# Neighbourhood attention on one core: two more tiles for turned probabilities, one store on another queue, and another split of V's shift

## The chip, the cores and the metric

The kernel runs on one core of a Trainium2 chip. The metric is the time of one execution on the device, in microseconds (us). Of the kernel before three runs are shown; their median is 342.44 us.

## The reference

The input is an image of 224 x 224 pixels with 192 channels in bfloat16. Each pixel attends to a 7 x 7 neighbourhood with a dilation of 2, clipped at the edges.

```python
qkv = x @ wqkv
r0 = jnp.clip(ir - half, 0, H - 1 - (ks - 1) * dil)      # ks 7, dil 2, half 6
c0 = jnp.clip(ic - half, 0, W - 1 - (ks - 1) * dil)
logits = jnp.einsum('bnc,bnkc->bnk', qf, kn) * scale     # kn, vn: keys and values of the 49 neighbours
p = _softmax(logits, axis=-1)
o = jnp.einsum('bnk,bnkc->bnc', p, vn) @ wo
```

## The kernel before

With a dilation of 2 a pixel only meets pixels of its own row parity and column parity. So the image falls into classes: the row class `rc` is 0 or 1, and the two column classes `cc` are worked on side by side. The work goes in 14 steps (`NSTEP`), for seven bands of 16 rows and the two row classes in turn. A step has seven pairs of slots; a slot is 16 rows by 8 columns, 128 queries of each column class. There are 98 pairs, counted by `k`; `n` is the step, `m` the pair in the step, `s = 2m` or `2m + 1` the slot (0 to 13).

The projections are folded together: G holds x times (wq wk^T), so that the scores are G against x itself, and V holds x times (wv wo), so that the last product is the output. Of the image, XA and XB hold channels and marks that make the softmax's window; x arrives by transposing DMAs (line 154), one third of it through the tiles of pool `x1` (two buffers), from which GpSimd copies it to XB (`xb_items`, line 160) and, sorted, to XS (`sort_items`, line 170).

A pair passes these stages:

- `stage1` (lines 499, 501): TensorE (PE) multiplies G with the window of x to scores in PSUM; VectorE (DVE) takes the negative maximum.
- `stage1b` (line 508): ScalarE (ACT) writes the exponentials, in bfloat16, to one of three tiles `p`.
- `stage2`: the probabilities are turned, to tile `pt_sb` (three buffers). Mostly PE does it (line 535) and DVE or ACT copies the result out of PSUM (line 536). The pairs in the table `TURN` are turned by a transposing DMA on SP's queue (line 519): the pair `m = 5` of steps 2 to 10, pairs 2 to 6 of steps 11 and 12, pairs 0 and 1 of step 13.
- `stage3` (line 545): PE multiplies the turned probabilities with V; a column of ones gives the sum.
- `stage4` (lines 551, 566, 568): DVE or ACT divides, and the output is stored (lines 574, 585, 597).

The order is written out by hand, and `in_order` keeps each engine's instructions in the order of the program. The loop over `k` emits `stage1` of pair k, then `stage3` and part of `stage4` of pair k - 3 (`values_of`), then the second half of `stage1b`, then `stage2` (at once for a pair turned by DMA, a pair later for the others).

Beside the pairs runs the work for the next step, by the tables `BACK` and, from k = 80 on, `LATE`: seven strings, one for each pair, naming blocks of V (`v0` to `v13`), parts of G (`g`) and the half parts of G (`h`), whose result GpSimd copies in place (line 450). The first entry of a string goes ahead of the second exponential, the others behind it.

V is kept twice: `stage3` of the upper half of the rows needs the lower half of V's partitions (0 to 63) in the other one of two tiles. `v_over` (line 349) copies it for a range of the 14 blocks. `back` calls it, when the block of a list has been made: after block 7 for blocks 0 to 7, after block 10 for 8 to 10, after block 13 for 11 to 13. It is a DMA on SP's queue, and in steps 11 and 12 (`nb >= 11`) a copy on GpSimd.

In the last step `stage4` puts the outputs of all slots into one tile (`xs`), and each slot from 1 on is stored with one DMA for 12 rows: slot 13 from ACT's queue, the others from SP's (line 574). The other four rows are stored as short stores over several slots (line 585): four on GpSimd after slot 7, four at the very end from the list `end_q`. GpSimd also stores slot 0 of every step in many small pieces (line 597), some of them after each pair.

SP's DMAs wait in order for what they need, and each also for the DMA eight places earlier, since eight semaphores go round.

Of the kernel before, what the change touches and what calls it, by code (L numbers as in the profile page):

```python
# [8 lines left out]
BF = mybir.dt.bfloat16  # L9
# [12 lines left out]
NSLOT = 14  # L22
# [5 lines left out]
BND = 16 * S  # L28
# [13 lines left out]
def _aff_runs(vals):  # L42
    out = []
    i, n = 0, len(vals)
    while i < n:
        j = i
        step = 1
        if i + 1 < n and vals[i + 1] > vals[i]:
            step = vals[i + 1] - vals[i]
            j = i + 1  # L50
            while j + 1 < n and vals[j + 1] - vals[j] == step:
                j += 1
        out.append((i, j - i + 1, vals[i], step))
        i = j + 1
    return out


def _rows(rc, ti):

    return [_phys(rc, 16 * ti + j) for j in range(16)]  # L60
# [7 lines left out]
def _win(t, p0, pn, off, dims):  # L68
    a = t[:]
    ps = a.ap[0][0]  # L70
    return bass.AP(a.tensor, a.offset + p0 * ps + off, [[ps, pn]] + [list(d) for d in dims])
# [18 lines left out]
def in_order(tc):  # L90

    last = {}
    for i in tc.nc.cur_bb.bb.instructions:
        if i.engine in last:
            tc.add_manual_dep(i, last[i.engine], mybir.DependencyInfo(mybir.DependencyClass.NoSync, mybir.DependencyReason.DATA), reason="program order")
        last[i.engine] = i.name
# [3 lines left out]
def kernel(  # L100
# [7 lines left out]
    nc = tc.nc  # L108
# [12 lines left out]
    x1_p = ctx.enter_context(tc.tile_pool(name="x1", bufs=2))  # L121
# [199 lines left out]
    work = ctx.enter_context(tc.tile_pool(name="work", bufs=2))  # L321
# [25 lines left out]
    def v_over(rc, ti, c0, c1, eng=nc.sync.dma_start):  # L347

        eng(out=VV[rc][1 - ti % 2][0:64, c0:c1, :], in_=VV[rc][ti % 2][0:64, c0:c1, :])
# [163 lines left out]
    def turned(J):  # L513
        return J.m in TURN[J.n]

    def stage2(J):
        J.pt = work.tile([128, 8, 128], BF, name="pt_sb", tag="pt_sb", bufs=3)
        if turned(J):
            nc.sync.dma_start_transpose(out=J.pt[:], in_=J.p[:].rearrange("p a c q k -> p (a c q k)"))
            return  # L520
        if J.k == NP - 1:

            for ab in range(2):
                pt_ps = ps_g.tile([128, 4, 128], BF, name="pt_ps", tag="pg")
                for i in range(4):
                    for h in range(2):
                        nc.tensor.transpose(pt_ps[64 * h:64 * h + 64, i, :], J.p[:, ab, i // 2, i % 2, 64 * h:64 * h + 64], ident[:])
                nc.vector.tensor_copy(out=J.pt[:, 4 * ab:4 * ab + 4, :], in_=pt_ps[:])
            return
        pt_ps = ps_t.tile([128, 8, 128], BF, name="pt_ps", tag="pt")  # L530
        for ab in range(2):
            for cc in range(2):
                for q in range(2):
                    for h in range(2):
                        nc.tensor.transpose(pt_ps[64 * h:64 * h + 64, 4 * ab + 2 * cc + q, :], J.p[:, ab, cc, q, 64 * h:64 * h + 64], ident[:])  # L535
        (nc.scalar.copy if J.n == NSTEP - 1 and 2 <= J.m < 5 else nc.vector.tensor_copy)(out=J.pt[:], in_=pt_ps[:])  # L536
# [12 lines left out]
    def stage4a(J, ab):  # L549
        J.rs[ab] = stat.tile([128, 2], F32, name="rs", tag="rs")  # L550
        nc.vector.reciprocal(out=J.rs[ab][:], in_=J.o_ps[ab][:, C:C + 2])  # L551
        return J.rs[ab]

    def stage4(J, ab):
        rc, ti, s, o_ps = J.rc, J.ti, 2 * J.m + ab, J.o_ps[ab]
        rs = J.rs.get(ab) or stage4a(J, ab)
        if s > 0 and J.n == NSTEP - 1:

            o_sb = _win(XS[0], 0, 128, 2 * C * s, [[C, 2], [1, C]])
        elif s > 0:  # L560
            o_sb = work.tile([128, 2, C], BF, name="o_sb", tag="o_sb", bufs=6)
        else:
            o_sb = work.tile([128, 2, C], BF, name="o_s0", tag="o_s0")
        if J.k >= NP - 3 and ab == 1:
            for cc in range(2):
                nc.scalar.mul(o_sb[:, cc, :], o_ps[:, 194 * cc:194 * cc + C], rs[:, cc:cc + 1])
        else:
            nc.vector.tensor_tensor(out=o_sb[:], in0=_win(o_ps, 0, 128, 0, [[194, 2], [1, C]]),  # L568
                                    in1=rs[:].unsqueeze(2).to_broadcast([128, 2, C]), op=ALU.mult)
        prow = _rows(rc, ti)  # L570
        if s > 0:
            for (j0, nj, r0, rstep) in _aff_runs(prow) if J.n < NSTEP - 1 else [(0, 12, prow[0], 2), (12, 1, prow[12], 1), (13, 3, prow[13], 2)]:
                def put(eng, j0=j0, nj=nj, r0=r0, rstep=rstep):
                    eng.dma_start(out=op[r0: r0 + (nj - 1) * rstep + 1: rstep, 8 * s - 3:8 * s + 5, :],
                                  in_=o_sb[8 * j0:8 * (j0 + nj)].rearrange("p t c -> p (t c)"))

                if J.n < NSTEP - 1:
                    put(nc.gpsimd if nj < 8 and s % 2 == 1 else nc.sync)
                elif nj >= 8:
                    put(nc.scalar if s == NSLOT - 1 else nc.sync)  # L580
                elif s in SHORT:

                    for j in range(nj):
                        def row(eng, p=8 * (j0 + j), r=r0 + j * rstep, a=SHORT[s]):
                            eng.dma_start(out=op[r, 8 * a - 3:8 * s + 5, :].rearrange("(t i) c -> i t c", i=8),
                                          in_=_win(XS[0], p, 8, 2 * C * a, [[2 * C, s + 1 - a], [1, 2 * C]]))
                        if s < NSLOT - 1:
                            row(nc.gpsimd)
                        else:
                            end_q.append(row)  # L590
            return
        for h in range(2):
            for (j0, nj, r0, rstep) in _aff_runs(prow[8 * h:8 * h + 8]):
                for (cc, i0, n, mem, pair) in ((0, 0, 3, 1, 0), (0, 3, 5, 0, 0), (1, 6, 2, 1, 3), (1, 0, 3, 1, 109), (1, 3, 3, 0, 109)):
                    p = 64 * h + 8 * j0 + i0 * nj
                    dst = op[r0: r0 + (nj - 1) * rstep + 1: rstep, pair:pair + n, mem * C:(mem + 1) * C]
                    pool_q.append(lambda dst=dst, p=p, m=n * nj, cc=cc: nc.gpsimd.dma_start(out=dst.rearrange("j i c -> i j c"), in_=o_sb[p:p + m, cc, :]))  # L597
# [3 lines left out]
    for n, (ti, rc) in enumerate(steps):  # L601
        for m in range(7):
            J = Pair()
# [94 lines left out]

    def back(it, by_dve):
        it(by_dve)  # L700
        for (i, c0, c1) in ((7, 0, 8), (10, 8, 11), (13, 11, 14)):
            if it in vs and it is vs[i]:
                v_over(rcb, tib, c0, c1, pool if nb >= 11 else nc.sync.dma_start)

# [6 lines left out]
    for k in range(NP + 2):  # L711
        J = pairs[k] if k < NP else None
# [21 lines left out]
        if k == NP:  # L734
            stage2(pairs[k - 1])
        late = [pairs[i] for i in values_of(k)]
        for A in late[:1]:
            stage3(A, 0)
            stage3(A, 1)
            if k >= NP:  # L740
                stage4a(A, 0)
                stage4a(A, 1)
            stage4(A, 0)
            if k == NP - 1:
                stage4a(A, 1)
        for (it, by_dve) in w64:
            back(it, by_dve)
        if J:
            stage1b(J, 1)
        if J and turned(J):  # L750
            stage2(J)
        if 1 <= k < NP and not turned(pairs[k - 1]):
            stage2(pairs[k - 1])

        if late and n > 0:
            stage4(late[0], 1)
        for A in late[1:]:
            stage3(A, 0)
            stage3(A, 1)
            stage4(A, 0)  # L760
            stage4(A, 1)
# [15 lines left out]
        for (it, by_dve) in w128:  # L777
            back(it, by_dve)
# [22 lines left out]
        pool_do(max(4 if n < NSTEP - 1 else 8, len(add)))  # L801
    pool_do(len(pool_q))
    for (q, it) in enumerate(end_q):
        it((nc.scalar, nc.sync)[q % 2])
    in_order(tc)


# [28 lines left out]
```

## Time and profile before

| | us |
|---|---|
| runs shown: lowest, median, highest | 341.17, 342.44, 344.3 |
| the profiled execution | 345.27 |
| its span, first to last instruction | 343.5 |
| mean granted clock of TensorE in it | 0.998 of full speed |

The span is the time between the first and the last instruction in the trace. A row of a group has the source line, engine, operation, tile written and tiles read, sizes, count, busy time, the mean of one, and the idle time before it with what ended it. A row of the timeline has start, time, engine, line and operation, and how many instructions are merged in it. SPq, ACTq and POOLq stand for the sequencers, which issue DMAs or wait. A row of waits has the engine and line that waited, what it waited for, the sum, the number of times and the longest.

### The profile page before, as it was taken

How to read it: one execution, taken by the hardware profiler on the slowest of the kernel's cores; microseconds unless marked ns; L12 is line 12 of the kernel's file. 1: busy time of each engine (PE TensorE's matmuls, PEld its weight loads, DVE VectorE, ACT ScalarE, POOL GpSimd, SP SyncE). 2: the span in 40 equal slices, each digit the busy share in tenths (PEclk: the TensorE clock that was granted, in tenths of full speed). 3: DMA queues.
4: the chain of work that ended last, by engine and by line, in shares of the span. 5: the costliest groups of instructions: out<-in, count | busy, mean ns of one | idle time of the engine just before them, and what ended most of it. 6: DMA issues, size and time to landing. Idle time of an engine off the chain costs nothing.

```text
span 343.5 us, 19147 instructions
## 1 busy us (share of the span) xinstructions
PE 321.3 (94%) x7964; PEld 295.1 (86%) x7964; DVE 311.4 (91%) x730; ACT 311.7 (91%) x816; POOL 288.2 (84%) x447
## 2 busy tenths in 40 slices
PE   4599999999999999999999999999999999899882
PEld 2478898899899999999999989899999999798771
DVE  8759999899999999989999999899999999799892
ACT  6679899999999999989999999999999999899982
POOL 8399999999989969699598895996969939998592
PEclk9999999999999999999999999999999999999999
DMA  8999645978999996896898979979898667769934
GB/s 173 212 169 209 132 100 123 223 177 195 181 177 167 175 195 155 160 196 141 165 173 166 202 160 165 155 164 176 178 193 182 138 136 119 140 112 111 174 87 98
DMA packets 135685, 55.43 MB, mean 161 GB/s; under 512 B 108717, under 2 KB 132826, under 8 KB 135599
## 3 DMA queue, kind: packets, MB, share of 16 engines
q1 hardware_dynamic: 129555, 51.63, 78.7%
q0 software_dynamic: 5328, 1.75, 2.9%
q8 instruction: 62, 1.02, 1.3%
q10 hardware_dynamic: 716, 0.84, 1.2%
q14 instruction: 24, 0.20, 0.2%
HBM read 0.29 MB, written 19.27 MB: 57 GB/s over the span
## 4 chain that ended last, share of the span: by engine, by line
PE 72%; ACT 7%; DMA 7%; DVE 6%; SPq 3%; issue 3%; DVEq 0%; ACTq 0%
PE s L499 16%; PE o_ps L545 15%; PE pg L415 11%; PE pv L335 8%; PE pt_ps L535 8%; PE pv L338 7%; PE pgh L415 6%; DMA pt_sb<-p 5%; ACT p L508 4%; SPq L154 3%; DVE nmx L501 3%; DMA xa<-in_x_dram 2%; ACT v L328 1%; ACT gx L328 1%; ACT g L328 1%
## 5 line engine op out<-in xcount | busy, mean ns | idle before, releaser
L508 ACT ACTIVATE p<-s,nmx 128x256 bf16<-128x256 f32 x392 | 163.1, 483 | 16.4 <-DVE nmx L501 14.1
L501 DVE TENSOR_REDUCE nmx<-s 128x2 f32<-128x448 f32 (+1 forms) x196 | 114.5, 624 | 12.1 <-PE s L499 6.9
L568 DVE TENSOR_TENSOR o_sb<-o_ps,rs 128x384 bf16<-128x384 f32 x169 | 94.2, 557 | 6.3 <-DVE rs L551 0.3
L499 PEld LDWEIGHTS <-g 128*64 128x64 bf16 x2592 | 86.8, 110 | 6.2 <-issue 2.7
L545 PE MATMUL o_ps<-v,pt_sb 128*64 128x193 bf16 x1568 | 87.3, 246 | 3.2 <-DMA pt_sb<-p 2.7
L450 POOL COPY g<-gx 64x512 bf16<-64x512 bf16 (+1 forms) x110 | 61.9, 563 | 33.2 <-ACT gx L328 28.9
L328 ACT CAST v<-pv 128x384 bf16<-128x384 f32 x180 | 85.7, 514 | 4.1 <-PE pv L338 3.8
L597 POOL DMA_DIRECT2D out_dram<-o_s x150 | 84.9, 572 | 1.4 <-DVE rs L551 1.4
L499 PE MATMUL s<-xa,g 128*64 128x196 bf16 (+8 forms) x1296 | 83.2, 217 | 1.8 <-issue 1.2
L499 PE MATMUL s<-xb,g 128*64 128x196 bf16 (+8 forms) x1296 | 83.0, 217 | 0.2 <-ACT g L328 0.2
L335 PE MATMUL pv<-wb,xs 128*64 128x384 bf16 x406 | 73.7, 331 | 3.8 <-POOL g L270 3.4
L545 PEld LDWEIGHTS <-pt_sb 128*64 128x64 bf16 x1568 | 71.2, 109 | 4.1 <-DMA pt_sb<-p 3.1
L338 PE MATMUL pv<-wp,xs 128*64 128x192 bf16 x812 | 74.1, 248 | 0.0
L338 PEld LDWEIGHTS <-xs 128*64 128x64 bf16 x812 | 60.0, 111 | 6.5
L415 PEld LDWEIGHTS <-aw 128*64 128x64 bf16 x1320 | 57.4, 110 | 7.5 <-issue 3.0
L328 ACT CAST g<-pg 128x512 bf16<-128x512 f32 (+4 forms) x139 | 60.6, 487 | 2.1 <-PE pg L415 1.5
L415 PE MATMUL pg<-xa,aw 128*64 128x512 bf16 (+9 forms) x440 | 53.4, 270 | 2.3 <-DMA xa<-in_x_dram 1.4
L415 PE MATMUL pg<-xb,aw 128*64 128x512 bf16 (+9 forms) x440 | 54.8, 269 | 0.0
L170 POOL COPY xs<-xa 128x896 bf16<-128x896 bf16 x51 | 46.6, 942 | 6.4 <-DMA xa<-in_x_dram 5.5
L535 PE MATMUL pt_ps<-ident,p 128*64 128x128 bf16 x1216 | 51.3, 219 | 0.0
L536 DVE COPY pt_sb<-pt_ps 128x1024 bf16<-128x1024 bf16 x73 | 49.7, 681 | 0.5 <-PE pt_ps L535 0.3
L535 PEld LDWEIGHTS <-p 128*64 128x64 bf16 x1216 | 45.0, 110 | 0.5
(73 smaller groups left out, 323.4 us busy)
## 6 DMA issues: line engine op xcount, KB each, us to landing
out_dram<-o_sb SPq DMA_DIRECT2D x156, 96.0 KB
v<-v SPq DMA_DIRECT2D x10, 386.0 KB
v<-v SPq DMA_DIRECT2D x22, 144.8 KB
out_dram<-o_s POOLq DMA_DIRECT2D x78, 9.0 KB, 3.8
out_dram<-o_sb SPq DMA_DIRECT2D x13, 78.0 KB
xb<-xb SPq DMA_DIRECT2D x2, 448.0 KB
out_dram<-xs SPq DMA_DIRECT2D x12, 72.0 KB
v<-v SPq DMA_DIRECT2D x2, 337.8 KB
```

The lines of the kernel that those rows point to most:

```text
L328: nc.scalar.copy(out=out_, in_=in_)
L335: nc.tensor.matmul(pv[64 * h:64 * h + 64, 0:2 * C], lhsT=at(1, h), rhs=WB[:].rearrange("p t c -> p (t c)"), start=True, stop=False, skip_g ...
L338: nc.tensor.matmul(pv[64 * h:64 * h + 64, cc * C:(cc + 1) * C], lhsT=at(2 * cc, h), rhs=WP[(cc, 0)], start=False, stop=True, skip_group_ch ...
L415: nc.tensor.matmul(o, lhsT=l, rhs=r, start=(pas == 0), stop=(pas == 1))
L450: nc.gpsimd.tensor_copy(out=G[rc][cc][p:p + 64, 1, s0:s0 + ns, :], in_=gx[p:p + 64, 0:ns * 128].rearrange("p (s q) -> p s q", q=128))
L499: nc.tensor.matmul(o, lhsT=w, rhs=r, start=(cc == 0 and done[h] == cols_), stop=(cc == 1 and not units[h]), skip_group_check=True)
L501: nc.vector.tensor_reduce(out=nmx[:], in_=_win(s_ps, 0, 128, lo, [[256, 2], [16, 16], [1, 16 - lo]]), axis=AX.XY, op=ALU.max, negate=True)
L508: nc.scalar.activation(out=J.p[:, ab, cc].rearrange("p q (r k) -> p q r k", k=8), in_=_win(s_ps, 0, 128, cc * 256, [[8, 2], [16, 16], [1, ...
L535: nc.tensor.transpose(pt_ps[64 * h:64 * h + 64, 4 * ab + 2 * cc + q, :], J.p[:, ab, cc, q, 64 * h:64 * h + 64], ident[:])
L545: nc.tensor.matmul(o_ps[64 * h:64 * h + 64, cc * 193:cc * 193 + 193], lhsT=J.pt[:, 4 * ab + 2 * cc + q, 64 * h:64 * h + 64], rhs=V[h][:, A ...
L568: nc.vector.tensor_tensor(out=o_sb[:], in0=_win(o_ps, 0, 128, 0, [[194, 2], [1, C]]), in1=rs[:].unsqueeze(2).to_broadcast([128, 2, C]), op ...
L597: pool_q.append(lambda dst=dst, p=p, m=n * nj, cc=cc: nc.gpsimd.dma_start(out=dst.rearrange("j i c -> i j c"), in_=o_sb[p:p + m, cc, :]))
```

## The change

Four places change. The tile of `stage2` comes, from pair 81 on (the fifth pair of step 11), for two of every five pairs from pool `x1`, whose two buffers hold no more of the image then; so five tiles are used in turn and not three. In the last step, slot 10's store is issued by GpSimd and not by SP. `back` shifts V's lower half in other portions: five blocks after block 4, five after block 9, four after block 13. Of the four short stores at the end three are now SP's and one, the second, is ACT's; it was two and two.

```diff
     def stage2(J):
-        J.pt = work.tile([128, 8, 128], BF, name="pt_sb", tag="pt_sb", bufs=3)
+        if J.k >= 81 and J.k % 5 in (0, 2):
+            J.pt = x1_p.tile([128, BND], BF, name="pt_x", tag="x1")[:, 0:1024].rearrange("p (a q) -> p a q", q=128)
+        else:
+            J.pt = work.tile([128, 8, 128], BF, name="pt_sb", tag="pt_sb", bufs=3)
         if turned(J):
...
                 elif nj >= 8:
-                    put(nc.scalar if s == NSLOT - 1 else nc.sync)
+                    put({NSLOT - 1: nc.scalar, NSLOT - 4: nc.gpsimd}.get(s, nc.sync))
...
         it(by_dve)
-        for (i, c0, c1) in ((7, 0, 8), (10, 8, 11), (13, 11, 14)):
+        for (i, c0, c1) in ((4, 0, 5), (9, 5, 10), (13, 10, 14)):
             if it in vs and it is vs[i]:
...
     for (q, it) in enumerate(end_q):
-        it((nc.scalar, nc.sync)[q % 2])
+        it((nc.sync, nc.scalar, nc.sync, nc.sync)[q])
```

In the order of the built program PE, DVE and ACT keep all their instructions in their places. On SP the first portion of V now stands just ahead of the turned transpose of steps 2 to 10, and the second just ahead of the load of x1. On GpSimd the first portion in steps 11 and 12 stands among the small stores of slot 0, ahead of the copies of `h2`, and slot 10's store is the last instruction that works.

## The prediction

> **What bounds the kernel now.** I read the page first, then the table of waits, then single stretches of the timeline. The page:
>
> ```profile
> span 343.5 us, 19147 instructions
> PE 321.3 (94%) x7964; PEld 295.1 (86%) x7964; DVE 311.4 (91%) x730; ACT 311.7 (91%) x816; POOL 288.2 (84%) x447
> PE 72%; ACT 7%; DMA 7%; DVE 6%; SPq 3%; issue 3%; DVEq 0%; ACTq 0%
> ```
>
> TensorE carries the chain that ends last (72%) and is busy 94% of the span. The view by stretches shows where the other 6% lie:
>
> ```profile
> 91.00:267.00 176.00, 174.80 (x4473) 164.05 (x4468) 166.37 (x386) 167.28 (x442) 148.62 (x209) 1.00 0.89 171
> 289.00:343.50 54.50, 43.92 (x1087) 39.23 (x1081) 43.96 (x111) 43.72 (x114) 41.78 (x71) 0.99 0.67 119
> ```
>
> The second number is the stretch, then PE's busy time; the last two are the DMA share and GB/s. From 91 to 267 us, eight steps, PE misses 1.2 us of 176: nothing can be won there, only lost. The diff does not touch the start (its first different order is the V shift of the second step). In the last 54.5 us PE misses 10.6, of which 6 to 7 are the tail behind its last matmul (ACT's last group of outputs, quoted below, starts at 336.53). The diff works in that last stretch and, with the V shift, on the DMA queues of the whole run. What PE waited for, and what SP's queue waited for:
>
> ```profile
> PE o_ps L545 <- DMA pt_sb<-p: 2.7, 3, 1.2
> PE s L499 <- issue: 1.2, 2, 0.7
> SPq L519 <- ACT p L508: 15.5, 9, 3.0
> 289.13 7.11 DMA pt_sb<-p
> 312.94 5.42 DMA pt_sb<-p
> 319.43 5.04 DMA pt_sb<-p
> ```
>
> The first three are rows of waits (us in total, times, the longest), the last three of the chain in order of time. Of 21 turned tiles three came late for PE, all after 289 us, for 2.7 us in sum; these are the ones that took 5.0 to 7.1 us from issue to landing.
>
> **Part 1, two more tiles for the turned probabilities.** PE, DVE and ACT keep their order and their number of working instructions; only the buffer changes, so that a tile is written again five pairs later and not three. That pays if a transpose on SP waits for `stage3` of three pairs earlier to have read the tile. It does not. The pair whose transpose was issued at 312.94:
>
> ```profile
> 308.57 0.85 PE L545 MATMUL o_ps<-v,pt_sb 128*64 128x193 bf16 x16
> 310.21 0.86 ACT L508 ACTIVATE p<-s,nmx 128x256 bf16<-128x256 f32 x2
> 308.74 2.82 SPq L519 DMA_TRANSPOSE pt_sb<-p  x1
> 311.65 1.19 SPq L574 DMA_DIRECT2D out_dram<-o_sb  x2
> 312.94 1.30 SPq L519 DMA_TRANSPOSE pt_sb<-p  x1
> ```
>
> PE had read the old tile by 309.42. The new probabilities were ready at 311.07 (310.21 + 0.86), 1.65 us later; and then SP, which had been issuing back to back since 308.74, reached the transpose 1.87 us after that. The reader of the old tile is never the last of the three. The order in the code says the same for every turned pair: `stage3(k-3)` stands ahead of the second exponential of pair k on PE and ACT. The table of waits puts SP's waits at L519 down to ACT, none to PE. So I cost this part at 0. Bounds: -2.7 us, if all of PE's waits for transposes went, and 0 above. The new wait is on GpSimd's sort, the last reader of the x1 buffers:
>
> ```profile
> 285.73 0.93 POOL L170 COPY xs<-x 128x896 bf16<-128x896 bf16 x1
> 297.96 0.69 DVE L536 COPY pt_sb<-pt_ps 128x1024 bf16<-128x1024 bf16 x1 [0.35 <-PE pt_ps L535]
> ```
>
> It ends at 286.66. The first instruction to wait for just that sort is DVE's copy into a pt_x tile in step 12, near 298: 11 us of room. The turned pair near 289 waits for a sort of a step earlier.
>
> **Part 2, V's lower half.** PE nowhere waits for this copy: the table of waits has no row for a reader of line 349. The copy costs SP three issues a step, before and after, and the same 14 blocks of data. What moves is the place. Before: eight blocks after block 7, then 3 and 3. After: five blocks after block 4, which stands on SP just ahead of the turned transpose of steps 2 to 10; five after block 9, just ahead of the load of x1; four at the end. Where SP is backlogged an issue has a pitch of 0.64 us (312.94 - 311.65 for two, above). In the DMA engines five blocks are 5/8 of 386.0 KB, 247,040 B.
>
> ```profile
> GB/s 173 212 169 209 132 100 123 223 177 195 181 177 167 175 195 155 160 196 141 165 173 166 202 160 165 155 164 176 178 193 182 138 136 119 140 112 111 174 87 98
> v<-v SPq DMA_DIRECT2D x10, 386.0 KB
> v<-v SPq DMA_DIRECT2D x22, 144.8 KB
> ```
>
> At the highest slice (223 GB/s) that is 1.1 us, at the mean 161 (the page's DMA line) 1.5 us. So the turned transpose lands up to 1.5 us later, and 2.2 where SP is backlogged. Its time to the first reader on PE, in the three tightest steps and a usual one:
>
> ```profile
> 89.15 1.38 SPq L519 DMA_TRANSPOSE pt_sb<-p  x1
> 94.62 0.25 PE L545 MATMUL o_ps<-v,pt_sb 128*64 128x193 bf16 x1
> 110.36 1.28 SPq L519 DMA_TRANSPOSE pt_sb<-p  x1
> 116.66 0.25 PE L545 MATMUL o_ps<-v,pt_sb 128*64 128x193 bf16 x1
> 223.23 1.27 SPq L519 DMA_TRANSPOSE pt_sb<-p  x1
> 229.29 0.25 PE L545 MATMUL o_ps<-v,pt_sb 128*64 128x193 bf16 x1
> 155.20 1.26 SPq L519 DMA_TRANSPOSE pt_sb<-p  x1
> 162.26 0.25 PE L545 MATMUL o_ps<-v,pt_sb 128*64 128x193 bf16 x1
> ```
>
> That is 5.47, 6.30, 6.06 and 7.06 us. No landing is shown for these; the three shown (5.0 to 7.1 us) are those that were too late, so the slowest of 21. I take 0, since the tiles that PE did not wait for landed sooner than those. Upper end: all landings at 5.42 plus 2.2 in the three tight steps, (7.62 - 5.47) + (7.62 - 6.30) + (7.62 - 6.06) = 5.0 us; the other six, not backlogged, 5.42 + 1.5 against some 7, are just in time. Lower end: -1.2, if the two issue gaps of PE at L499 (fetching behind big transfers would look so) went with the eight-block burst.
>
> The Trainium skill, DMA: Bandwidth & Descriptors, section Queues, rings and completion order, says that each DMA engine takes turns between queues packet by packet, but consumes one queue's descriptors in order. By that rule the transpose, on the same SP queue, pays for V's whole block and not a share of it. No row here shows the order inside a queue; the rule weighs for the upper end just given.
>
> In steps 11 and 12 this copy is GpSimd's:
>
> ```profile
> L349 POOL COPY v<-v x6: 1145/1147/2757, 294.3 to 323.8; 64x1158 bf16<-64x1158 bf16 x4, 64x3088 bf16<-64x3088 bf16 x2
> 288.42 4.49 POOL L597 DMA_DIRECT2D out_dram<-o_s  x8
> 292.95 1.28 POOL L450 COPY g<-gx 64x512 bf16<-64x512 bf16 x2
> ```
>
> (2757 - 1147)/5 = 322 ns for a block: 1.79, 1.79 and 1.47 us after, 2.76, 1.15, 1.15 before, 5.05 both. The first copy now stands among the eight stores, so that four stores and the two copies of g behind it come 1.8 us later (292.95 to 294.7); their readers are the next step's fifth and sixth pairs, over 10 us on. The copy behind them gets shorter and takes it back. The last is 0.32 longer and lies before an idle stretch. Cost 0.
>
> **Part 3, the tail.** Slot 10's store leaves SP for GpSimd; of the last four short stores SP now takes three and ACT one.
>
> ```profile
> 336.99 0.77 SPq L574 DMA_DIRECT2D out_dram<-xs  x1
> 337.86 0.77 SPq L574 DMA_DIRECT2D out_dram<-xs  x1
> 338.73 0.77 SPq L574 DMA_DIRECT2D out_dram<-xs  x1
> 339.60 0.77 SPq L585 DMA_DIRECT2D out_dram<-xs  x2
> 336.53 1.47 ACT L566 ACTIVATE xs<-o_ps,rs 128x192 bf16<-128x192 f32 x4 [0.82 <-DVE rs L551]
> 334.89 2.41 POOL L585 DMA_DIRECT2D out_dram<-xs  x4
> L831 POOLq DRAIN  x3: 40/93/5605, 335.9 to 343.2; - x3
> L831 SPq DRAIN  x3: 7/7/7, 342.7 to 343.0; - x3
> ```
>
> The stores at 336.99, 337.86 and 338.73 are slots 10, 11, 12, a pitch of 0.87. Without the first, slot 11 waits for its data (ACT, half of 1.47 from 336.53: 337.27) and starts at 337.3, slot 12 at 338.2, the short stores at 339.05, 339.5 and 339.85, the last done at 340.2. Before, it was done at 340.37. So 0.87 us off SP brings 0.2: 0.31 go to the wait for slot 11's data, and 0.35 to the third short store, which ACT had. What follows the last issue stays. On GpSimd the store comes after 337.30 and takes 0.6 us (2.41/4), or 1.05 if it goes by pieces (96 against 56). The drain of GpSimd ended at 341.5; 0.6 to 1.05 later is 342.1 to 342.55, still ahead of SP's at 342.7 less 0.2, or level with it. I take -0.2, with ends -0.9 and +0.3.
>
> **Sum.** 0 + 0 - 0.2. The profiled execution took 345.27 us around its span of 343.5; less 0.2, 345.1. It lies 2.8 above the median of the runs shown, 342.44, so I carry the difference over: 342.2.
>
> **Rivals.** (a) *Slower: late transposes in steps 2 to 10.* The five-block shift ahead of the turned transpose makes PE wait at L545 around 94, 116 and 229 us. For it: SP's order, and 89% DMA share. Against it: no such wait now. Price 5.0: 342.2 + 5.0 = 347.2. It decides from a delay that eats the room of the 5.47 us step, and costs over 1% only if the three together wait over 3.6 us. (b) *Faster: PE's late waits go.* The extra tiles or the better-spread V blocks take away all 2.7 us at L545 and the 1.2 at L499: 342.2 - 3.9 = 338.3. For it: the three waits are where the tiles are added. Against it: the wait runs from issue to landing, and the tile's old reader was done before. The Trainium skill, Perfetto Trace Analysis, section DMA Optimizations, says that splitting transfers may let the work finish sooner where DMA engines are generally idle. By it the split of V would help here by these same waits; with a share of 0.89 they are not idle, so the trace does not grant the condition. (c) *GpSimd ends the kernel*: its drain, 4.2 us behind its last store's 337.30, moves behind SP's: 342.2 + 0.5 = 342.7.
>
> **How the numbers follow.** Forecast 0.72, (c) 0.09, (a) 0.10, (b) 0.09. Some 1% is what a measurement here can tell from no change. Forecast and (c) are within it: 0.81; (a) gives slower 0.10, (b) faster 0.09. The range leaves (a) and (b) out, their smaller forms in: the runs shown go from 341.17 to 344.3; with the tail's -0.9 below that, 340.2, and its +0.3 above, 344.6.
>
> **What would show it.** Right: PE's waits for pt at L545 remain, two to four, and the transposes there still follow ACT's or SP's own backlog; no wait of PE before 289 us for pt; the third of SP's last L585 stores starts near 339.85; the last GpSimd store near 337.3. Wrong: waits at L545 before 280 us (a), or none after 289 (b); or a GpSimd drain after SP's (c).

## The result, and the profile after

The changed kernel is slower: 344.78 us against 342.63, medians of 22 runs each, ratio 1.0052 (95% interval 1.0031 to 1.0072). I had predicted 342.2 and a range up to 344.6. In twelve of the changed kernel's executions the granted clock of TensorE was 0.985 to 0.992, with a median of 345.6 us; in the ten others it was 0.994 to 0.998, with 343.5, which is 0.8 above the median of before. The profiled executions mislead if their spans are compared: the one of before (345.27 us) is 2.6 above its median, the one of after (343.35 around a span of 341.6) is 1.4 below its own. Both profiles have a clock of 0.998. So I compare stretches, not ends. Lines of `kernel.py` behind 517 are three higher after the change: 545 is 548, 574 is 577, 585 is 588, 519 is 522.

The view by stretches (us from the start, length, busy time of PE, PEld, DVE, ACT and POOL, then clock, DMA share, GB/s), first a row of before that was not shown yet:

```profile
47.00:91.00 44.00, 43.88 (x1070) 39.97 (x1067) 40.45 (x95) 42.65 (x114) 42.66 (x65) 1.00 0.83 177
```

and the changed kernel:

```profile
47.00:91.00 44.00, 41.57 (x1018) 38.37 (x1014) 38.34 (x88) 40.98 (x109) 42.51 (x65) 1.00 0.87 175
91.00:267.00 176.00, 175.69 (x4489) 164.77 (x4486) 167.16 (x389) 168.18 (x445) 145.66 (x205) 1.00 0.88 172
289.00:341.60 52.60, 44.30 (x1107) 40.24 (x1102) 44.45 (x112) 43.91 (x115) 42.80 (x74) 0.98 0.68 126
```

Between 47 and 91 us, two steps in which PE had been idle for 0.12 us, it is now idle for 2.43. The long middle loses nothing. One row of the changed kernel's waits (us in total, times, longest) names the place, and the timeline around it shows it:

```profile
PE o_ps L548 <- DMA v<-v: 2.3, 1, 2.3
```

```profile
46.33 0.54 ACTq L349 DMA_DIRECT2D v<-v  x1
49.85 0.85 PE L548 MATMUL o_ps<-v,pt_sb 128*64 128x193 bf16 x16
51.95 0.56 SPq L349 DMA_DIRECT2D v<-v  x1
55.23 0.86 PE L548 MATMUL o_ps<-v,pt_sb 128*64 128x193 bf16 x16 [2.30 <-DMA v<-v]
```

The same stretch of the kernel before:

```profile
46.99 0.54 ACTq L349 DMA_DIRECT2D v<-v  x1
50.51 0.85 PE L545 MATMUL o_ps<-v,pt_sb 128*64 128x193 bf16 x16
53.43 0.83 PE L545 MATMUL o_ps<-v,pt_sb 128*64 128x193 bf16 x16
57.63 0.56 SPq L349 DMA_DIRECT2D v<-v  x1
```

The DMA on ACT's queue is the copy of blocks 0 to 7 at the end of step 0 (the last entries of `PLAN`), which belongs to step 1's V and stands outside `back`. Before, the next copy, of blocks 8 to 10, went out at 57.63, behind the first `stage3` of step 1 at 53.43. After, `back` shifts blocks 5 to 9 as soon as block 9 is there, at 51.95: it rewrites blocks 5, 6 and 7, which had been shifted already, and it does so ahead of that `stage3`. The first pair of step 1 reads block 7: slot 0 needs column block 13, which the table `AT` keeps at place 7. So PE waits until the second copy has landed, for bytes that the first had brought. The pairs behind it are held up as much: from VectorE's first maximum of the pair k = 9 to that of the next pair it takes 5.73 us (52.83 to 58.56), before 3.26 (53.49 to 56.75).

### The profile page after: what moved, and what is told of

It reads as the page before. It is cut to its first block, busy times and chain, and to the rows that moved or that the text cites. A ratio compares the mean times of both kernels' runs of the same rounds, so it can differ in the third digit from the quotient of the medians.

```text
span 341.6 us, 19157 instructions
## 1 busy us (share of the span) xinstructions
PE 321.9 (94%) x7964; PEld 296.6 (87%) x7964; DVE 311.2 (91%) x730; ACT 311.4 (91%) x816; POOL 288.1 (84%) x448
## 4 chain that ended last, share of the span: by engine, by line
PE 77%; ACT 8%; DVE 5%; DMA 4%; SPq 3%; issue 1%; ACTq 0%; DVEq 0%
PE s L499 17%; PE o_ps L548 16%; PE pg L415 12%; PE pv L335 9%; PE pt_ps L538 8%; PE pv L338 8%; PE pgh L415 6%; ACT p L508 4%; SPq L154 3%; DVE nmx L501 2%; DMA pt_sb<-p 2%; DMA xa<-in_x_dram 1%; ACT v L328 1%; DMA v<-v 1%; ACT gx L328 1%
## 5 line engine op out<-in xcount | busy, mean ns | idle before, releaser
L548 PE MATMUL o_ps<-v,pt_sb 128*64 128x193 bf16 x1456 | 81.9, 246 | 3.9 <-DMA v<-v 2.3
L335 PE MATMUL pv<-wb,xs 128*64 128x384 bf16 x406 | 74.7, 333 | 3.6 <-ACT xs L360 3.1
L338 PE MATMUL pv<-wp,xs 128*64 128x192 bf16 x812 | 75.2, 250 | 0.0
L548 PEld LDWEIGHTS <-pt_sb 128*64 128x64 bf16 x1456 | 66.7, 109 | 4.9 <-issue 2.4
L338 PEld LDWEIGHTS <-xs 128*64 128x64 bf16 x812 | 61.3, 111 | 6.2
L539 DVE COPY pt_sb<-pt_ps 128x1024 bf16<-128x1024 bf16 x72 | 49.0, 681 | 0.9 <-PE pt_ps L538 0.8
```

What stands on the lines that cost most here:

```text
L335: nc.tensor.matmul(pv[64 * h:64 * h + 64, 0:2 * C], lhsT=at(1, h), rhs=WB[:].rearrange("p t c -> p (t c)"), start=True, stop=False, skip_g ...
L338: nc.tensor.matmul(pv[64 * h:64 * h + 64, cc * C:(cc + 1) * C], lhsT=at(2 * cc, h), rhs=WP[(cc, 0)], start=False, stop=True, skip_group_ch ...
L548: nc.tensor.matmul(o_ps[64 * h:64 * h + 64, cc * 193:cc * 193 + 193], lhsT=J.pt[:, 4 * ab + 2 * cc + q, 64 * h:64 * h + 64], rhs=V[h][:, A ...
```

## The experiments

Theory A: this overlap, and the one wait that it makes, is the loss. Rival B: V's new portions cost time in steps 2 to 10, by late turned tiles. Rival C: the two tiles or the tail cost it. The ratios are each to the kernel before on the same chip.

**The changed kernel without the overlap.**

```diff
-        for (i, c0, c1) in ((4, 0, 5), (9, 5, 10), (13, 10, 14)):
+        for (i, c0, c1) in (((9, 8, 10), (13, 10, 14)) if nb == 0 else ((4, 0, 5), (9, 5, 10), (13, 10, 14))):
```

> The changed kernel whole, except that for the first V built beside the pairs (for step 1) the portion after block 9 holds blocks 8 and 9 alone and not 5 to 9; blocks 5 to 7 were shifted already by the copy of blocks 0 to 7 at the end of step 0. Theory A (overlap: the second copy rewrites block 7, which the first pair of step 1 reads, so PE waits once, 2.3 us in the changed kernel's trace): the wait near 55 us goes, and the time is that of the kernel before less 0.2 to 0 us, ratio 0.998 to 1.001. Rival B (V's portions ahead of the turned transposes and of the loads cost time in steps 2 to 10): stays slower, ratio 1.004 to 1.006. Rival C (the two more tiles or the tail cost the time): the same, 1.004 to 1.006.

Measured 341.17 us, ratio 0.998 (0.996 to 0.9999). The copy still goes out at the same place, and PE does not wait:

```profile
51.13 0.57 SPq L349 DMA_DIRECT2D v<-v  x1
52.90 0.83 PE L548 MATMUL o_ps<-v,pt_sb 128*64 128x193 bf16 x16
```

Three blocks less in one copy of some forty turn a loss of 0.5% into a gain of 0.2%. Of all kernels here this is the quickest, and the only one whose interval lies wholly under 1, if only just. The time is as theory A expected; rivals B and C, which expected 1.004 to 1.006, are outside the interval.

**V's portions alone**, on the kernel before:

```diff
-        for (i, c0, c1) in ((7, 0, 8), (10, 8, 11), (13, 11, 14)):
+        for (i, c0, c1) in ((4, 0, 5), (9, 5, 10), (13, 10, 14)):
```

> The kernel before with the new portions of V alone (five, five, four; step 1 included). Theory A: PE waits near 55 us by 2 to 2.5 us for the copy of V, and the time is 1.8 to 2.4 us above before, ratio 1.005 to 1.007. Rival B: the same ratio, but the time is lost in waits for turned tiles between 90 and 280 us. Rival C: no change, 0.999 to 1.001.

Measured 344.30 us from six runs, ratio 1.0071 (1.0047 to 1.0095): the whole loss and no other part needed. PE's waits for turned tiles are 0.5 us in this trace, which is too little for it, and the timeline has the wait for V again:

```profile
51.60 0.56 SPq L349 DMA_DIRECT2D v<-v  x1
55.64 0.86 PE L545 MATMUL o_ps<-v,pt_sb 128*64 128x193 bf16 x16 [2.14 <-DMA v<-v]
```

**V's portions from step 2 on**, with the old ones for step 1 (here and in the next two runs only the new line is shown; it replaces the same old one):

```diff
+        for (i, c0, c1) in (((7, 0, 8), (10, 8, 11), (13, 11, 14)) if nb == 0 else ((4, 0, 5), (9, 5, 10), (13, 10, 14))):
```

> The kernel before with the new portions of V from the second V on (for steps 2 to 13), the first V (for step 1) in the old portions 8, 3, 3. Theory A: no wait near 55 us, the ratio 0.999 to 1.002; PE may wait 0 to 0.5 us in sum for turned tiles before 280 us. Rival B: 1.004 to 1.006, with those waits at 1.5 us or more.

Measured 342.53 us, ratio 1.0015 (0.9991 to 1.0039). Without the portion of step 1 no loss can be told. Rival B's mechanism exists, at a seventh of the 5.0 us that the prediction priced it at, and a little above the 0 to 0.5 us expected here: PE waited for turned tiles at 139 and 206 us, where it had not before.

```profile
PE o_ps L545 <- DMA pt_sb<-p: 0.7, 2, 0.5
```

**Block 7 a second time**, and nothing else, on the kernel before:

```diff
+        for (i, c0, c1) in (((9, 7, 8), (10, 8, 11), (13, 11, 14)) if nb == 0 else ((7, 0, 8), (10, 8, 11), (13, 11, 14))):
```

> The kernel before, with one more copy of V: for step 1, after block 9, block 7 alone is shifted a second time (64 partitions of 772 bytes). Nothing else is moved. Theory A: PE waits for this small copy at the first pair of step 1 almost as long as in the changed kernel, since issue to landing is mostly fixed time: 1.3 to 2.0 us, ratio 1.004 to 1.006. Rivals B and C: so small a copy costs nothing, 0.999 to 1.001.

```profile
50.98 0.56 SPq L349 DMA_DIRECT2D v<-v  x1
54.54 0.86 PE L545 MATMUL o_ps<-v,pt_sb 128*64 128x193 bf16 x16 [1.71 <-DMA v<-v]
```

A copy of 772 bytes in each of 64 partitions, a fifth of the new portion, makes PE wait 1.71 us. In the stage it shows whole: from the first maximum of k = 9 to the next pair's it takes 5.14 us, in the seven traces without this wait 3.24 to 3.26. The time was 343.04 us, ratio 1.0025 (1.0003 to 1.0047), slower as theory A says, but by 0.9 us (0.1 to 1.6) and so less than the wait in its profile; the 1.004 expected is within the interval, and so is the 1.001 of the rivals. The time alone decides little here, the trace does. Stretches that no edit touches vary as much: from k = 28 to k = 42 six kernels that are alike there took 45.26 to 46.92 us. Whether this is why the time shows only part of the wait stays open.

**Blocks 5 and 6 a second time**, at the same place, not block 7. This sets the reader's wait against rival D, that the rewriting or the extra DMA as such costs:

```diff
+        for (i, c0, c1) in (((9, 5, 7), (10, 8, 11), (13, 11, 14)) if nb == 0 else ((7, 0, 8), (10, 8, 11), (13, 11, 14))):
```

> The kernel before, with one more copy of V at the same place as in the run with block 7: for step 1, after block 9, blocks 5 and 6 are shifted a second time, block 7 is not. Their first readers are the third and fourth pair of step 1 and not the first. Theory A (the wait of the first pair for block 7 is the cost): no wait of PE at line 545 near 54 us, ratio 0.999 to 1.001. Rival D (rewriting shifted blocks, or one more DMA on SP's queue at this place, is the cost, whoever reads): 1.003 to 1.006.

```profile
51.23 0.56 SPq L349 DMA_DIRECT2D v<-v  x1
52.98 0.83 PE L545 MATMUL o_ps<-v,pt_sb 128*64 128x193 bf16 x16
```

Measured 342.19 us, ratio 0.9988 (0.9969 to 1.0007). Twice the data of the run before, at the same place on the same queue, costs nothing that these runs can tell: rival D, which expected 1.003 or more, falls. What counts is that the block has a reader before the copy has landed.

**The tiles alone** (only the hunk in `stage2`):

> The kernel before with the two more tiles for turned probabilities alone. Theory A: the tile was never what the transposes waited for; SP's waits at this line stay with ACT, and the ratio is 0.998 to 1.002. Rival C (the tiles help or harm): outside that, by the 2.7 us that PE waited for turned tiles in the trace of before, 0.992, or harm, 1.004.

Measured 342.38 us, ratio 0.999 (0.9967 to 1.0013). SP's queue waits at the turning line with or without the tiles; here its largest entry there is

```profile
SPq L522 <- ACT p L508: 10.7, 7, 3.0
```

and no entry names PE. One row is new, and it comes in the four traces with the tiles and in no other: the view has SP wait there once for GpSimd (line 450), for 1.0 us here and for 0.7 to 2.4 in the others. No wait of PE for one of the two new tiles follows in any of them.

**The tail alone** (the hunks of slot 10's store and of `end_q`):

> The kernel before with the tail's change alone: slot 10's store on GpSimd, three short stores on SP and one on ACT. Theory A: from PE's last matmul to the last issue's end 0.2 us less than the 3.4 before, ratio 0.998 to 1.001. Rival (GpSimd ends the kernel): its drain ends after SP's, ratio 1.001 to 1.002.

Measured 342.44 us, ratio 0.9993 (0.9967 to 1.002). A gain of 0.2 us, 0.06%, can't be told from none in such runs. The traces tell it: from the start of ACT's last outputs to the end of SP's last issue it takes 3.64 to 3.68 us in the four kernels with the new tail (3.68 here, 333.76 to 337.44), and 3.82 to 3.96 in the six without. From the end of PE's last matmul it is 3.25 us here and 3.41 before. The rival is out in this trace: GpSimd's long drain is over at 339.35, and SP's first comes at 339.62.

**Tiles and tail, V as before:**

> The kernel before with tiles and tail, V's portions as before. Theory A: as the tail alone, ratio 0.998 to 1.001, and level with the changed kernel without the overlap (0.998), so that V's portions of steps 2 to 13 are worth nothing either way. If those portions are a gain of their own, this one is over 0.999 and that one stays below.

Measured 341.88 us, ratio 0.9993 (0.9968 to 1.0019). The changed kernel without the overlap has 0.998 (0.996 to 0.9999); the intervals cover each other, so whether V's portions of steps 2 to 13 bring anything stays open, within some 0.3%; the run with these portions alone (1.0015) shows no gain.

## Why the prediction was wrong

**The step that failed** is the sentence at the head of part 2, that PE nowhere waits for this copy, so that only its effect on queues and DMA engines had to be priced. It was read from the waits of before, and true there. But a wait that is missing says only that the copy came early enough at its old place, or that the reader had gone by. I moved the copy and priced its neighbours on SP, without asking for each portion who reads it next at the new place. Nor did I look at what it covers: my first paragraph set the start aside, because the first different order is the second V's shift, and that is just the place where the loss is. `PLAN` had shifted blocks 0 to 7 for step 1 already; with the old list `back` then added blocks 8 to 10 and 11 to 13, which fits; with the new one it adds 5 to 9 and 10 to 13. So part 2's "the same 14 blocks" is wrong for step 1 too: it is 17. The term was 0 and measured 2.3 us in the trace of the changed kernel; with the tail's -0.2 this gives 2.1, and the runs say 1.8 (1.1 to 2.5, from the ratio). That the two agree may be partly chance: the ten executions at the higher clock lie only 0.8 above before, near the 0.9 of the run with block 7, and the rest comes with the lower clock. Whether the wait brings that clock on stays open. The comparison behind the result has no clocks of before; in the experiments all 64 executions of before were at 0.993 or more, one of six with V's portions alone was at 0.989 and one of twelve with the portions from step 2 on at 0.992. The range ended 0.2 below the measured median, since none of my rivals held this wait.

**Tiles: right.** The runs with the tiles alone show neither gain nor harm, and SP's waits at the turning line stay with ACT, but for the one on GpSimd, which the prediction did not expect of a turned pair; no wait of PE for one of the new tiles follows it. The three late tiles of before, 2.7 us in sum, were no feature of the kernel: in the changed kernel there are two in the same stretch, and with the tiles alone PE's matmuls have no such wait at all, while the run with blocks 5 and 6, which has no more tiles than before, has none either. Over the ten traces PE's waits for turned tiles behind 289 us are 2.7 us in before, 0.8 in the changed kernel and 0.2 or less in the others, so they come and go; 2.7 is about what before's profiled execution lay above its median. The changed kernel's row:

```profile
PE o_ps L548 <- DMA pt_sb<-p: 0.8, 2, 0.4
```

**V's portions in steps 2 to 10: taken as 0, and nearly so.** The changed kernel's waits have no turned tile before 289 us; its one short stop at such a place, 0.31 us at 141.34, the view puts down to PE itself. But rival (a)'s mechanism is there: in the other three traces with these portions PE waited for one or two such tiles before 289 us, by 0.2 to 0.7 us in sum, and in the six traces without them for none. The block stands ahead of the turned transpose; here is the longest case, from the run with the portions from step 2 on, the third row being the landing in its chain:

```profile
131.88 0.55 SPq L349 DMA_DIRECT2D v<-v  x1
132.53 1.39 SPq L519 DMA_TRANSPOSE pt_sb<-p  x1
132.53 6.66 DMA pt_sb<-p
139.36 0.86 PE L545 MATMUL o_ps<-v,pt_sb 128*64 128x193 bf16 x16 [0.52 <-DMA pt_sb<-p]
```

From issue to reader 6.83 us, and 0.52 of them idle. It is not one of the three steps that I had named as tight; of those only the one near 229 us waited, in two of the traces (0.20 and 0.17 us). The Trainium skill's rule in DMA: Bandwidth & Descriptors, section Queues, rings and completion order, that each DMA engine consumes a queue's descriptors in order, fits this delay, but no row shows it by itself.

**The tail: right, with its size.** SP's last stores in the changed kernel, ACT's outputs, GpSimd's last store and the drains:

```profile
335.76 0.77 SPq L577 DMA_DIRECT2D out_dram<-xs  x1
336.63 0.77 SPq L577 DMA_DIRECT2D out_dram<-xs  x1
337.50 1.14 SPq L588 DMA_DIRECT2D out_dram<-xs  x3
335.00 1.47 ACT L569 ACTIVATE xs<-o_ps,rs 128x192 bf16<-128x192 f32 x4 [0.82 <-DVE rs L554]
335.80 0.60 POOL L577 DMA_DIRECT2D out_dram<-xs  x1
L834 POOLq DRAIN  x3: 40/93/4950, 335.7 to 341.3; - x3
L834 SPq DRAIN  x3: 7/7/7, 340.7 to 341.1; - x3
```

From the start of ACT's last outputs to the end of SP's last issue: 338.64 - 335.00 = 3.64 us, before 340.37 - 336.53 = 3.84. Slot 11's store starts 0.76 after ACT's start, as worked out (0.77), and the store on GpSimd took 0.60. GpSimd's long drain ends at 340.65 (335.70 + 4.95), SP's first drain comes at 340.7: rival (c) missed by some 0.1 us in this trace. Whether a second store on GpSimd there would be paid for, no run shows.

## What to carry to other kernels

Before a copy is moved or cut anew, list for each piece who reads it next at its new place, and whether another copy already brings the same bytes: a rewrite that is harmless to the result makes a reader wait again if it comes before the copy has landed. That a view of waits has no row for a producer holds for its old place only. And look first where a loop's table meets a special case (here the hand-written start that does a part of the loop's work), since a new table must fit that too.

## What was not expected of the hardware

How long the copy takes, between two places in SBUF, hardly depends on its size. From issue to landing, in the chains of the changed kernel (five blocks), of V's portions alone (five) and of block 7 again (one):

```profile
51.95 3.15 DMA v<-v
51.60 3.90 DMA v<-v
50.98 3.42 DMA v<-v
```

From SP's issue to PE's first matmul it was 3.28, 4.04 and 3.56 us. And PE's waits for turning DMAs near the end were 2.7 us in one execution of before, and 0.2 and none in two kernels alike in that stretch (block 7 again, blocks 5 and 6 again), which is more than any part of this change was meant to move.
